# Buffers of a second matrix stage rotated in order of use, its memory laid out anew, weight preparation split in two

## The chip, the cores and the metric

The kernel runs on one core of one Trainium2 chip. The metric is the time of one execution in device microseconds, from the first to the last work of that core; a kernel's time is the median of its runs. Lower is better. Engines are named as in the profile: PE (matrix engine; PEld is its weight load), DVE (vector), ACT (scalar), POOL (GpSimd), SP (the engine that issues the transfers).

## The reference

An attention over pooled keys and values feeds two feed-forward layers. Both layers have 4608 tokens, a model width of 512 and a hidden width of 2048; they differ in the function between their two matrix products.

```python
def reference(q, k, v, ...):
    k_p, v_p = mean over groups of 8 rows of k, v          # (8, 8, 72, 64)
    attn = softmax(q @ k_p.T / sqrt(64)); x = attn @ v_p    # -> (4608, 512)
    h = x @ moe_w_in                                        # (4608, 2048)
    g = where(h >= 1, h, where(h <= -1, 0, (h + 1) ** 2 / 4))
    x = g @ moe_w_out                                       # (4608, 512)
    h = x @ moe2_w_in
    g = h - tanh(h)
    return g @ moe2_w_out                                   # (4608, 512)
```

## The kernel before

Every matrix operand is held as a pair, a rounded high part and the rest as a low part, and a product is three matmuls (high by high, high by low, low by high) added up in PSUM.

**First part.** The tokens go through in 12 blocks of 384. A block has 16 steps, one for each 128 hidden rows: `h_mm` makes the hidden values, DVE and ACT apply the function and split the result into `gh` and `gl`, and `out_mm` adds their product, two steps later, into four PSUM banks. Beside that run the attention of later blocks (names `pkt`, `psc`, `pam`, `ah`, `al`, `rr`; `al` is a DVE subtraction that frees the PSUM buffer that `pkt` and others use next) and, in steps of 8, `w2_prep`, which prepares the weights of the second layer. For an even unit, POOL forms four sums `c1` to `c4` of quarters of the first weight matrix, ACT and DVE split sums and quarters into high and low (L237, L238), and DMAs write them to memory as `w2c`; an odd unit gives `w2o`. The order of this part's engines is found by a scheduler that places the instructions by its own estimate of when they can run; POOL, ACT, DVE and SP each work off their queue strictly in that order.

**Second part.** 9 blocks J of 512 tokens by 8 pairs p of 256 hidden rows make 72 steps n = 8J + p. The first matrix product of a step is done in seven products of quarter size (`product(n, m)`, six matmuls of 256 columns each, in the order m = 1, 6, 7, 2, 5, 4, 3) into three PSUM banks `bkA`, `bkX`, `bkZ`. ACT and DVE combine them (`v_s`, `v_w`, `v_z`, `v_c11`, `v_t`, `v_c22`, `v_c21`, `v_c12`) into two halves: half 1 is complete after product 4, half 0 after product 3. On each half follow `v_th` (tanh, ACT), `v_sub` (DVE), `v_hi` (high part `gh`, ACT) and `v_lo` (low part `gl`, DVE), and `o_mm(n, half)`, 12 matmuls of 512 columns that add to the output banks `y0` to `y3`. `o_mm` of step n - 1 stands in PE's queue between the products of step n: half 1 before product 3, half 0 after it.

The order of the second part is a table of times (`at_time`) that is sorted; times are only the sorting key. `c`, `gh` and `gl` have three buffers each, and half h of step n takes buffer (2n + h) mod 3, while in every step half 1 is made and used first. So `v_hi(n, 1)` writes the buffer that half 0 of step n - 1 has, since (2n + 1) and 2(n - 1) differ by 3, and waits until `o_mm(n - 1, 0)`, the last matmuls of step n on PE, have read it.

Loads of the second part stand in SP's one queue: `xr` (the tokens of a block, converted by `xc_hi` on ACT and `xc_lo` on DVE into seven operands `xc`), `wc0` to `wc7` (1792 KB each, product weights of pair p, loaded once) and `wr` (512 KB each, weights of one `o_mm`, four buffers). Its memory is one pool per tag, laid out in the order of `LAYOUT` over the memory of the first part, and each tile waits only for those tiles of the first part that lie where it lies.

## Time and profile before

| what | us |
|---|---|
| median of 3 runs | 2015.25 (2009.29 to 2019.15) |
| the profiled execution | 2020.92 |
| its span, first to last instruction | 2018.8 |
| end of the first part on PE | about 992 |
| PE busy in the span | 1821.6 (90%) |

All rows below are from the one profiled execution, and their times count from its first instruction. The granted clock (PEclk) is 1.00 when TensorE had 2.4 GHz and 0.50 when it had 1.2 GHz for the whole stretch. A row of the timeline gives start, duration, engine, line, and in brackets the idle time ahead with what ended it. Durations of matmuls include the time in which their result drains, so that rows that follow each other overlap; the distance between starts is what PE spends.

### The profile page before, as it was taken

The numbers are of one execution on the slowest core, as the hardware profiler recorded it, in microseconds if no ns is written. First come the engines' busy times: TensorE is split into PE (matmuls) and PEld (weight loads), VectorE is DVE, ScalarE is ACT, GpSimd is POOL, SyncE is SP. The second block draws the span as 40 slices with busy tenths as digits, with TensorE's granted clock in tenths as the row PEclk, the third lists the DMA queues.
The fourth block names the chain that finished last, engine by engine and source line by source line (L and its number), as shares of the span: only waits on it lengthen the run. The fifth ranks groups of instructions, "written<-read, shape, count | busy, mean of one in ns | idle before, by whom it ended". The sixth has DMA issues, their size and how long they took to land.

```text
span 2018.8 us, 27653 instructions
## 1 busy us (share of the span) xinstructions
PE 1821.6 (90%) x10224; PEld 1657.9 (82%) x10224; DVE 1060.2 (53%) x1993; ACT 804.0 (40%) x2014; POOL 333.1 (17%) x433
## 2 busy tenths in 40 slices
PE   8999999999999999999858888888888888888888
PEld 6579999999999999999847777777777777777776
DVE  8878667666667665554413434343433334343433
ACT  6656555555555544443312323232322223232322
POOL 4442333223331242011010101001010101000000
PEclk8999999999999999999979999899989899999899
DMA  7623334233343231102362323123232323232222
GB/s 229 235 75 111 119 93 149 69 97 128 100 122 95 85 114 50 24 10 74 140 236 84 109 79 125 63 94 113 71 120 73 115 84 105 84 125 73 94 75 71
DMA packets 162423, 207.60 MB, mean 103 GB/s; under 512 B 77808, under 2 KB 115696, under 8 KB 161264
## 3 DMA queue, kind: packets, MB, share of 16 engines
q1 hardware_dynamic: 162288, 205.84, 31.4%
q8 instruction: 80, 1.31, 0.3%
q14 instruction: 55, 0.45, 0.1%
HBM read 163.32 MB, written 41.94 MB: 102 GB/s over the span
## 4 chain that ended last, share of the span: by engine, by line
PE 69%; DVE 12%; ACT 10%; DMA 3%; issue 3%; POOL 2%; SPq 0%; ACTq 0%; DVEq 0%; POOLq 0%
PE y L986 20%; PE po L617 15%; PE ph L572 14%; PE bkX L921 7%; ACT gh L970 4%; PE bkZ L921 3%; PE bkA L921 3%; DVE gl L974 3%; DVE c L964 2%; ACT th L961 2%; DMA wr<-w2o 2%; PE psc L431 2%; PE ph L565 1%; DVE c L957 1%; DVE gl L596 1%
## 5 line engine op out<-in xcount | busy, mean ns | idle before, releaser
L986 PE MATMUL y<-wr,gh 128*128 128x512 f32 x1152 | 370.1, 403 | 22.5 <-DMA wr<-w2o 22.0
L974 DVE TENSOR_TENSOR gl<-c,gh 128x512 fp32r<-128x512 f32 x144 | 104.2, 724 | 412.0 <-ACT gh L970 412.0
L921 PE MATMUL bkA<-xc,wc 128*128 128x256 f32 x864 | 144.3, 307 | 142.3 <-ACT s L933 140.7
L986 PEld LDWEIGHTS y<-wr,gh 128*128 128x128 f32 x1152 | 214.4, 196 | 63.2 <-DMA wr<-w2o 22.2
L921 PEld LDWEIGHTS bkA<-xc,wc 128*128 128x128 f32 x864 | 125.3, 202 | 163.3 <-ACT s L933 155.3
L970 ACT ACTIVATE gh<-c 128x512 fp32r<-128x512 f32 x144 | 90.8, 631 | 421.0 <-PE y L986 365.6
L986 PE MATMUL y<-wr,gl 128*128 128x512 f32 x576 | 229.2, 398 | 0.0
L921 PE MATMUL bkX<-xc,wc 128*128 128x256 f32 x1296 | 217.7, 309 | 3.0 <-DVE c L943 1.2
L921 PEld LDWEIGHTS bkX<-xc,wc 128*128 128x128 f32 x1296 | 194.4, 212 | 20.1 <-DVE c L943 12.8
L572 PE MATMUL ph<-xh,whl 128*128 128x384 f32 x704 | 200.3, 345 | 0.0
L583 ACT ACTIVATE g<-g,half 128x384 f32<-128x384 f32 x192 | 118.6, 618 | 199.6 <-DVE g L579 195.4
L617 PE MATMUL po<-gh,whl 128*128 128x384 f32 x704 | 196.7, 340 | 0.0
L961 ACT ACTIVATE th<-c 128x512 f32<-128x512 f32 x144 | 91.0, 632 | 245.1 <-DVE c L954 162.4
L596 DVE TENSOR_TENSOR gl<-g,gh 128x384 fp32r<-128x384 f32 x176 | 113.7, 646 | 81.7 <-ACT gh L595 79.4
L888 POOL TENSOR_TENSOR xr<-xr 128x512 f32<-128x512 f32 x9 | 11.6, 1290 | 863.7 <-DMA xr<-x2d 863.7
L964 DVE TENSOR_TENSOR c<-c,th 128x512 f32<-128x512 f32 x144 | 99.8, 693 | 99.8 <-ACT th L961 99.8
L579 DVE TENSOR_SCALAR g<-ph 128x384 f32<-128x384 f32 x192 | 106.2, 553 | 77.4 <-PE ph L572 70.7
L921 PE MATMUL bkZ<-xc,wc 128*128 128x256 f32 x864 | 146.2, 312 | 0.0
L587 DVE TENSOR_TENSOR g<-ph,g 128x384 f32<-128x384 f32 x192 | 106.4, 554 | 70.7 <-ACT g L583 68.7
L921 PEld LDWEIGHTS bkZ<-xc,wc 128*128 128x128 f32 x864 | 134.3, 224 | 0.0
L986 PEld LDWEIGHTS y<-wr,gl 128*128 128x128 f32 x576 | 110.2, 191 | 27.6 <-DVE gl L974 0.9
L572 PEld LDWEIGHTS ph<-xh,whl 128*128 128x128 f32 x704 | 130.9, 191 | 0.3
(156 smaller groups left out, 3642.2 us busy)
## 6 DMA issues: line engine op xcount, KB each, us to landing
wr<-w2o SPq DMA_DIRECT2D x144, 512.0 KB, 3.3
wraw<-in_moe_w_in_dram SPq DMA_DIRECT2D x32, 512.0 KB, 3.8
wraw<-in_moe_w_out_dram SPq DMA_DIRECT2D x32, 512.0 KB, 4.5
wc<-w2c SPq DMA_DIRECT2D x8, 1792.0 KB, 11.3
x2d<-ost SPq DMA_DIRECT2D x48, 192.0 KB, 1.9
out_dram<-yo SPq DMA_DIRECT2D x36, 256.0 KB, 2.2
w2c<-wraw SPq DMA_DIRECT2D x16, 512.0 KB, 2.6
kvraw<-in_k_dram SPq DMA_DIRECT2D x28, 256.0 KB, 2.8
```

The lines of the kernel that those rows point to most:

```text
L572: nc.tensor.matmul(ps, a[:, cs], x[:, c, :], start=(i == 0), stop=(i == 3 * KC - 1))
L579: nc.vector.tensor_scalar(a, hp[t], -1.0, 1.0, ALU.max, ALU.min)
L583: nc.scalar.activation(a, a, AF.Square, bias=half, scale=0.5)
L587: nc.vector.tensor_tensor(a, hp.pop(t), a, ALU.max)
L596: nc.vector.tensor_tensor(gl, a, gh.bitcast(F32), ALU.subtract)
L617: nc.tensor.matmul(o, a, m, start=(f == 0 and i == 0), stop=(f == FC - 1 and i == len(ops) - 1))
L921: nc.tensor.matmul(o, w[:, wi, c], x[:, xi, c], start=new and i == 0, stop=i == 5, skip_group_check=not new)
L961: nc.scalar.activation(th, H[(n, i)], AF.Tanh)
L964: nc.vector.tensor_tensor(H[(n, i)], H[(n, i)], GG.pop((n, i, "t")), ALU.subtract)
L970: nc.scalar.activation(gh, H[(n, i)], AF.Copy)
L974: nc.vector.tensor_tensor(gl, H.pop((n, i)), gh.bitcast(F32), ALU.subtract)
L986: nc.tensor.matmul(Y[c], a[:, cs], b, start=first and i == 0, stop=last and i == 2)
```

## The change

The rotation index of `c`, `gh` and `gl` becomes (2n + 1 - h) mod 3. `LAYOUT` puts the tags in another order, so that each lies over other tiles of the first part. The times at which `xr`, `wc`, `wr` and the first conversions are sorted in are new. `w2_prep` ends after POOL's sums, a new `w2_split` with the split and the DMAs follows two steps later, and the load of the next unit comes one step after that. As built, the seven `xc` now lie over first-part weights of hidden rows 8 to 11 (128 rows each), and their first conversions stand ahead of the last two steps' `gh` on ACT and `gl` on DVE; `wc0` lies over the constants, among them `half`, which every step's Square (L583) reads.

```diff
--- before.py
+++ after.py
@@ -231,6 +231,18 @@
             conv(r[:, i], a[:, i], r[:, i, :, 0])
         af = a.bitcast(F32)
         r0, r1 = (r[:, i].rearrange("p m t -> p (m t)") for i in (0, 1))
+        U[("w2", u)] = (r, af, r0, r1)
+        if u % 2:
+            return
+        a11, a12, a21, a22 = (af[:, i, 256 * c : 256 * c + 256] for i in (0, 1) for c in (0, 1))
+        c1, c2, c3, c4 = (r0[:, 256 * i : 256 * i + 256].bitcast(F32) for i in range(4))
+        nc.gpsimd.tensor_tensor(c1, a21, a22, ALU.add)
+        nc.gpsimd.tensor_tensor(c3, a11, a21, ALU.subtract)
+        nc.gpsimd.tensor_tensor(c2, c1, a11, ALU.subtract)
+        nc.gpsimd.tensor_tensor(c4, a12, c2, ALU.subtract)
+
+    def w2_split(u):
+        r, af, r0, r1 = U.pop(("w2", u))
         p = u // 2
 
         def split(x, hi):
@@ -244,12 +256,6 @@
                 nc.sync.dma_start(out=w2o[2 * p + i][:, 0], in_=hi)
                 nc.sync.dma_start(out=w2o[2 * p + i][:, 1], in_=lo)
             return
-        a11, a12, a21, a22 = (af[:, i, 256 * c : 256 * c + 256] for i in (0, 1) for c in (0, 1))
-        c1, c2, c3, c4 = (r0[:, 256 * i : 256 * i + 256].bitcast(F32) for i in range(4))
-        nc.gpsimd.tensor_tensor(c1, a21, a22, ALU.add)
-        nc.gpsimd.tensor_tensor(c3, a11, a21, ALU.subtract)
-        nc.gpsimd.tensor_tensor(c2, c1, a11, ALU.subtract)
-        nc.gpsimd.tensor_tensor(c4, a12, c2, ALU.subtract)
         split(af.rearrange("p i m -> p (i m)"), r1)
         for x, h in ((af.rearrange("p i m -> p (i m)"), 1), (r1.bitcast(F32), 0)):
             nc.sync.dma_start(out=w2c[p][:, h, 4:6], in_=x[:, 0:512].rearrange("p (m n) -> p m n", n=256))
@@ -805,7 +811,8 @@
             ahead("w", w_load, (1, f))
         t = FC + 8 * f + 5
         add(t, "w", w2_prep, f)
-        add(t + 1, "load2", used, "w")
+        add(t + 2, "w", w2_split, f)
+        add(t + 3, "load2", used, "w")
 
     def go(t, *slots):
         for s in slots:
@@ -847,8 +854,8 @@
     NPR = FC // 2
     TAGS = {}
     LAYOUT = (
-        "xc0 xc1 xc2 s0 s1 z0 w3 w4 r0 p640 w0 xc3 xc4 t0 w1 gh0 gh1 gh2 gl0 gl1 gl2 c0 c1 c2 xc5 t1"
-        " y0 y1 y2 y3 p1024 xr p1728 w6 w7 r1 w2 w5 r2 r3 xc6"
+        "w0 s0 p640 xc0 xc5 xc6 xc1 xc4 xc3 xc2 s1 z0 c0 w1 w2 r0 c1 c2 gh0 gh1 gh2 gl0 gl1 gl2 t0 t1 w5"
+        " y0 y1 p1024 xr p1728 w6 w7 y2 y3 w3 w4 r1 r2 r3"
     )
     for x in LAYOUT.split():
         TAGS[x] = one_pool(f"two_{x}", reuse_waits="tile")
@@ -925,7 +932,7 @@
 
     def tile_of(n, half):
         if (n, half) not in H:
-            H[(n, half)] = two(f"c{(2 * n + half) % 3}", [P, T2], F32, "c")
+            H[(n, half)] = two(f"c{(2 * n + 1 - half) % 3}", [P, T2], F32, "c")
         return H[(n, half)]
 
     def v_s(n):
@@ -964,7 +971,7 @@
         nc.vector.tensor_tensor(H[(n, i)], H[(n, i)], GG.pop((n, i, "t")), ALU.subtract)
 
     def v_hi(n, i):
-        k = (2 * n + i) % 3
+        k = (2 * n + 1 - i) % 3
         gh = two(f"gh{k}", [P, T2], F32R, "gh2")
         GG[(n, i)] = (gh, two(f"gl{k}", [P, T2], F32R, "gl2"))
         nc.scalar.activation(gh, H[(n, i)], AF.Copy)
@@ -1005,18 +1012,16 @@
     L = 10.4
     NS = NJ * NPR
     WHEN = {1: 0.0, 6: 0.7, 7: 1.4, 2: 2.1, 5: 2.8, 4: 3.5, 3: 6.95}
-    at_time(-60, xr_load, 0)
-    for i, p in enumerate((0, 1)):
-        at_time(-50 + i, wc_load, p)
-    at_time(-48, xr_sums, 0)
-    for i, m in enumerate(ORDER):
-        at_time(-47 + i, xc_hi, 0, m)
-        at_time(-46.5 + i, xc_lo, 0, m)
-    for i, p in enumerate(range(2, NPR)):
-        at_time(-30 + 4 * i, wc_load, p)
     fs = [2 * (n % NPR) + h for n in range(NS) for h in (1, 0)]
-    for i in range(4):
-        at_time(-5 + i, wr_load, fs[i])
+    at_time(-85, xr_load, 0)
+    at_time(-70, xr_sums, 0)
+    for p, t in enumerate((-80, -60, -55, -44, -34, 0, 8, 22)):
+        at_time(t, wc_load, p)
+    for i, t in enumerate((-54, -29, -28, -27)):
+        at_time(t, wr_load, fs[i])
+    for m, t in zip(ORDER, (-22, -21, -16, -15, -11, -10, -6)):
+        at_time(t, xc_hi, 0, m)
+        at_time(t + 0.6, xc_lo, 0, m)
     for n in range(NS + 1):
         J, p = divmod(n, NPR)
         b = n * L
```

ACT in a middle step of the second part, from `v_s` to the next step's `v_s`, with the engines that each row waits for. Before:

```order
L933 ACTIVATE s<-bkA 128x256 [waits PE_49]
L937 ACTIVATE z<-bkZ 128x256 [waits PE_49]
L940 ACTIVATE c<-bkA 128x256 [waits PE_49]
L961 ACTIVATE th<-c 128x512 [waits DVE_49,Activation_49]
L970 ACTIVATE gh_11746<-c 128x512 [waits DVE_49,PE_49]
L961 ACTIVATE th<-c 128x512 [waits DVE_49,Activation_49]
L970 ACTIVATE gh_11774<-c 128x512 [waits DVE_49]
L933 ACTIVATE s<-bkA 128x256 [waits PE_49]
```

After:

```order
L940 ACTIVATE s<-bkA 128x256 [waits PE_49]
L944 ACTIVATE z<-bkZ 128x256 [waits PE_49]
L947 ACTIVATE c<-bkA 128x256 [waits PE_49,Activation_49]
L968 ACTIVATE th<-c 128x512 [waits DVE_49]
L977 ACTIVATE gh_11746<-c 128x512 [waits DVE_49]
L968 ACTIVATE th<-c 128x512 [waits DVE_49,Activation_49]
L977 ACTIVATE gh_11774<-c 128x512 [waits DVE_49,PE_49]
L940 ACTIVATE s<-bkA 128x256 [waits PE_49]
```

The wait of the first `gh` (half 1) for PE has moved to the second `gh` (half 0).

SP from the load of `wc0` on, at the end of the first part (`x2d11` are the first part's last stores). Before, with the four first `wr` loads behind the last row shown:

```order
L868 DMA wc0_10510<-w2c0_84 128x3584 [waits DMAHW7_49,PE_49]
L627 DMA x2d11_119<-ost_10358 128x384 [waits DMAHW0_49,Activation_49]
L627 DMA x2d11_119<-ost_10358 128x384 [waits DMAHW1_49,DVE_49]
L627 DMA x2d11_119<-ost_10358 128x384 [waits DMAHW2_49,Activation_49]
L627 DMA x2d11_119<-ost_10358 128x384 [waits DMAHW3_49,DVE_49]
L868 DMA wc1_10512<-w2c1_85 128x3584 [waits DMAHW4_49]
L868 DMA wc2_10539<-w2c2_86 128x3584 [waits DMAHW5_49,PE_49]
L868 DMA wc3_10541<-w2c3_87 128x3584 [waits DMAHW6_49,PE_49]
L868 DMA wc4_10543<-w2c4_88 128x3584 [waits DMAHW7_49,PE_49]
L868 DMA wc5_10545<-w2c5_89 128x3584 [waits DMAHW0_49]
L868 DMA wc6_10547<-w2c6_90 128x3584 [waits DMAHW1_49,PE_49]
L868 DMA wc7_10549<-w2c7_91 128x3584 [waits DMAHW2_49,PE_49]
```

After:

```order
L875 DMA wc0_10510<-w2c0_84 128x3584 [waits DMAHW7_49,Activation_49]
L633 DMA x2d11_119<-ost_10358 128x384 [waits DMAHW0_49,Activation_49]
L633 DMA x2d11_119<-ost_10358 128x384 [waits DMAHW1_49,DVE_49]
L633 DMA x2d11_119<-ost_10358 128x384 [waits DMAHW2_49,Activation_49]
L633 DMA x2d11_119<-ost_10358 128x384 [waits DMAHW3_49,DVE_49]
L875 DMA wc1_10516<-w2c1_85 128x3584 [waits DMAHW4_49,PE_49]
L875 DMA wc2_10518<-w2c2_86 128x3584 [waits DMAHW5_49,PE_49]
L914 DMA wr_10520<-w2o1_93 128x1024 [waits DMAHW6_49]
L875 DMA wc3_10522<-w2c3_87 128x3584 [waits DMAHW7_49,PE_49]
L875 DMA wc4_10524<-w2c4_88 128x3584 [waits DMAHW0_49,PE_49]
L914 DMA wr_10526<-w2o0_92 128x1024 [waits DMAHW1_49]
L914 DMA wr_10528<-w2o3_95 128x1024 [waits DMAHW2_49,PE_49]
```

`wr` loads stand between the `wc` loads now, and `wc0` waits for ACT, the engine of the first part's last reader of its memory, instead of PE.

DVE in the first part around an even unit of `w2_prep` (L238 before, L250 after, is the split's subtraction; `g` and `gl` belong to the step's function). Before:

```order
L238 TENSOR_TENSOR wf<-wf,wraw 128x1024 [waits Activation_49,Pool_49]
L596 TENSOR_TENSOR gl<-g,gh 128x384 [waits Activation_49]
L579 TENSOR_SCALAR g<-ph 128x384 [waits PE_49]
L587 TENSOR_TENSOR g<-ph,g 128x384 [waits Activation_49]
L596 TENSOR_TENSOR gl<-g,gh 128x384 [waits Activation_49]
L579 TENSOR_SCALAR g<-ph 128x384 [waits PE_49]
L238 TENSOR_TENSOR wraw<-wraw 128x1024 [waits Activation_49]
L587 TENSOR_TENSOR g<-ph,g 128x384 [waits Activation_49]
L504 CAST ar_132<-par 16x128 [waits Activation_49]
L511 TENSOR_TENSOR al<-pam,ah 128x384
```

After:

```order
L250 TENSOR_TENSOR wf<-wf,wraw 128x1024 [waits Activation_49,Pool_49]
L602 TENSOR_TENSOR gl<-g,gh 128x384 [waits Activation_49]
L585 TENSOR_SCALAR g<-ph 128x384 [waits PE_49]
L593 TENSOR_TENSOR g<-ph,g 128x384 [waits Activation_49]
L602 TENSOR_TENSOR gl<-g,gh 128x384 [waits Activation_49]
L585 TENSOR_SCALAR g<-ph 128x384 [waits PE_49]
L517 TENSOR_TENSOR al<-pam,ah 128x384 [waits Activation_49]
L593 TENSOR_TENSOR g<-ph,g 128x384 [waits Activation_49]
L510 CAST ar_132<-par 16x128 [waits Activation_49]
L250 TENSOR_TENSOR wraw<-wraw 128x1024 [waits Activation_49]
```

The first subtraction, with its wait for POOL, stands where it stood; the second has moved behind `al`.

## Rows read from the trace of the kernel before

**Rows 1.** The page, busy time of PE: busy, share of the span, instructions.
```profile
PE 1821.6 (90%) x10224; PEld 1657.9 (82%) x10224; DVE 1060.2 (53%) x1993; ACT 804.0 (40%) x2014; POOL 333.1 (17%) x433
```

**Rows 2.** Stretches: length, then busy time (instructions) of PE, PEld, DVE, ACT, POOL; granted clock, DMA share, GB/s.
```profile
350.00:400.00 50.00, 50.00 (x300) 49.58 (x299) 32.20 (x66) 24.52 (x77) 13.56 (x20) 1.00 0.20 56
483.00:486.00 3.00, 3.00 (x11) 3.00 (x11) 1.39 (x5) 1.07 (x4) 1.22 (x4) 0.50 0.44 156
1010.00:1020.00 10.00, 0.00 (x0) 0.00 (x0) 0.00 (x0) 0.00 (x0) 0.00 (x0) 0.60 1.01 429
```

**Rows 3.** Waits of PE from 150 to 900: for whom, total us, times, longest.
```profile
PE pkt L350 <- DVE al L511: 12.2, 8, 2.8
PE psc L431 <- DVE al L511: 2.5, 2, 2.3
```

**Rows 4.** Timeline of DVE from 236 to 248, an even unit: start, us, what, [idle before].
```profile
237.32 1.23 DVE L238 TENSOR_TENSOR wf<-wf,wraw 128x1024 fp32r<-128x1024 f32 x1 [3.41 <-POOL wraw L252]
243.21 1.22 DVE L238 TENSOR_TENSOR wraw<-wraw 128x1024 fp32r<-128x1024 f32 x1
245.24 0.56 DVE L511 TENSOR_TENSOR al<-pam,ah 128x384 fp32r<-128x384 f32 x1
```

**Rows 5.** Timeline of SP's queue at the change of parts.
```profile
993.01 3.82 SPq L868 DMA_DIRECT2D wc<-w2c  x7
996.88 12.60 SPq L907 DMA_DIRECT2D wr<-w2o  x4
```

**Rows 6.** Timelines of ACT and PE at the change of parts.
```profile
986.74 0.62 ACT L583 ACTIVATE g<-g,half 128x384 f32<-128x384 f32 x1 [2.49 <-DVE g L579]
991.92 3.22 ACT L895 ACTIVATE xc<-xr 128x512 fp32r<-128x512 f32 x6
1000.68 0.95 PE L921 MATMUL bkA<-xc,wc 128*128 128x256 f32 x6 [1.55 <-DMA wc<-w2c]
1029.22 1.22 PE L986 MATMUL y<-wr,gh 128*128 128x512 f32 x2 [21.99 <-DMA wr<-w2o]
1033.55 0.88 PE L921 MATMUL bkX<-xc,wc 128*128 128x256 f32 x6
```

**Rows 7.** The line of the wc loads: time from issue to landing.
```profile
DMA to landing us min/median/max: 7.0/11.3/20.4
```

**Rows 8.** Timeline of PE in a middle step of the second part.
```profile
1505.45 0.86 PE L921 MATMUL bkX<-xc,wc 128*128 128x256 f32 x6
1506.15 0.63 PE L986 MATMUL y<-wr,gh 128*128 128x512 f32 x2
1508.95 0.86 PE L921 MATMUL bkA<-xc,wc 128*128 128x256 f32 x6
1513.05 1.16 PE L921 MATMUL bkA<-xc,wc 128*128 128x256 f32 x6 [1.82 <-ACT s L933]
1514.06 1.65 PE L921 MATMUL bkX<-xc,wc 128*128 128x256 f32 x6
1516.79 0.77 PE L986 MATMUL y<-wr,gh 128*128 128x512 f32 x2
1523.23 0.87 PE L921 MATMUL bkA<-xc,wc 128*128 128x256 f32 x6
```

**Rows 9.** Timeline of ACT in the same step.
```profile
1523.20 0.63 ACT L970 ACTIVATE gh<-c 128x512 fp32r<-128x512 f32 x1 [5.02 <-PE y L986]
1526.37 0.63 ACT L970 ACTIVATE gh<-c 128x512 fp32r<-128x512 f32 x1 [0.76 <-DVE c L964]
1526.91 0.37 ACT L933 ACTIVATE s<-bkA 128x256 f32<-128x256 f32 x1
```

**Rows 10.** Waits of PE from 1110 to the end: for whom, total us, times, longest.
```profile
PE bkA L921 <- ACT s L933: 129.6, 65, 2.8
```

**Rows 11.** Groups of DVE from 1100 to 1900: count, then busy us, mean ns of one, idle before.
```profile
L964 DVE TENSOR_TENSOR c<-c,th 128x512 f32<-128x512 f32 x116 | 80.4, 693 | 78.6 <-ACT th L961 78.6
L957 DVE TENSOR_TENSOR c<-bkX,s 128x256 f32<-128x256 f32 x58 | 24.2, 417 | 0.0
```

**Rows 12.** Timeline of PE: first product of steps 2 and 71, and the last matmul.
```profile
1037.06 0.86 PE L921 MATMUL bkA<-xc,wc 128*128 128x256 f32 x6
1993.67 0.87 PE L921 MATMUL bkA<-xc,wc 128*128 128x256 f32 x6
2014.69 0.39 PE L986 MATMUL y<-wr,gl 128*128 128x512 f32 x1
```

## Prediction

> **What bounds the kernel now.** I read the page first, then stretches of the span, then in each part what PE waits for. PE is busy 90% of the span [rows 1], so the question is where the other tenth lies and what PE spends at half clock. There are three places. In the first part PE is almost never idle and its clock stays at 1.00 (2.4 GHz) where it is not [rows 2]; its waits from 150 to 900 are nearly all for one subtraction, `al`, 12.2 + 2.5 us, the longest 2.8 [rows 3], and after such a wait the clock falls to 0.50 (1.2 GHz) [rows 2]. At the change of parts PE waits 21.99 us for the first `wr`, with no matmul at all from 1010 to 1020 while the transfers run at 429 GB/s [rows 2, 6]. In the second part, the largest place, PE waits 129.6 us in 65 of the steps for `s` on ACT [rows 10], and the clock falls again after these waits.
>
> **One step of the second part.** The period of the step shown is 1523.23 - 1508.95 = 14.28 us [rows 8]. From starts at full clock, a product costs 1506.15 - 1505.45 = 0.70 and an `o_mm` 1508.95 - 1506.15 = 2.80, so the matmuls of a step need 7 x 0.70 + 2 x 2.80 = 10.50. The rest is the wait of 1.82 before the second matmul group of `bkA`, and the half clock behind it: 1516.79 - 1514.06 = 2.73 for two products that need 1.40. Why is `s` late? ACT could make it 0.86 after the step's start, when the first product has drained, but in its queue stand `gh` of half 1, tanh and `gh` of half 0 of the step before. That first `gh` waited 5.02 us for PE, until 1523.20 [rows 9], which is the end of the last `o_mm` (1523.23 is the next start, [rows 8]): it wants the buffer that this `o_mm` reads. From there a chain of `gh`, `gl`, `c12`, tanh, `v_sub`, `gh` runs to 1526.91, when `s` starts, and PE stands. It closes every step: the period is the PE work up to the last `o_mm` plus this chain. From step 2 to step 71 the mean is (1993.67 - 1037.06) / 69 = 13.86 [rows 12].
>
> **The rotation, part by part.** With the index (2n + 1 - h) mod 3 the buffers follow each other in the order of use, and the writer of one meets the user three halves back. I walk one step from its start at 0, with 0.15 for the draining of a product (0.86 against 0.70, [rows 8]), 0.63 for tanh and `gh`, 0.37 for `s` [rows 9], 0.69 for a DVE subtraction of 512 columns and 0.42 for one of 256 [rows 11]. Six products start at 0, 0.70, 1.40, 2.10, 2.80, 3.50; `o_mm` of half 1 at 4.20, product 3 at 7.00, `o_mm` of half 0 at 7.70, next step at 10.50. `s` 0.86 to 1.23, wanted by the fourth product at 2.10. `w` 1.56 to 1.98, wanted at 2.80. `t` ends at 4.08, wanted at 7.00. `c22` ends at 4.50, `c21` at 4.92, tanh 5.55, subtraction 6.24, `gh` of half 1 at 6.87: its buffer was last read by an `o_mm` that ended at 0. `gl` 7.56. Product 3 drained at 7.85, `c12` 8.27, tanh 8.90, subtraction 9.59, `gh` of half 0 at 10.22: its wait for PE is new, but that `o_mm` ended at 7.00, so it costs nothing. Behind it in ACT's queue is the next `s`, wanted at 10.50 + 0.86 = 11.36: 1.1 us to spare. `gl` ends at 10.91 on DVE, where the next `w` is wanted at 12.06: 1.1 to spare. Nothing is late next; PE is the bound, and without its waits the clock should stay where it is from 350 to 400, at 1.00 with PE busy for all 50 us [rows 2]. So 10.50 a step. The slack is what hides two extra loads: in each block's last step seven conversions on ACT and seven on DVE (0.54 each on ACT, 3.22 for six, [rows 6]; on DVE at most 0.69), in its first step two copies on each. They bring the margins near zero, and POOL's sums slow DVE at times; I allow 6 us for the 8 changes of block. Gain: 69 x (13.86 - 10.50) = 232 less 6 = **226**. Bounds: 240 (nothing of the allowance and 0.1 less a step) and 200 (0.35 more a step, a third of the slack used up as waiting). Behind step 71 PE now needs 2014.69 + 0.39 - 1993.67 = 21.4 [rows 12]; it will need 10.50 + 2 x 2.80 = 16.1: **5.3** more.
>
> **The change of parts.** Seven `wc` are issued from 993.01 and the four `wr` behind them [rows 5]; `wc1` is there when PE goes on at 1000.68, the first `wr` at 1029.22 [rows 6]. Between lie 6 x 1792 + 512 = 11264 KB in 28.54 us, 395 KB a us, and they come in the order of their issue. After the change the first `wr` has one `wc` between it and `wc1`: 2304 KB, 5.8 us, at 1006.5. PE has the six products of step 1 until about 1007.5 (step 0 has no `o_mm` that would cover its chain, as before), so this wait is gone. The second `wr` has two more `wc` ahead: 4096 KB, 10.4 us, at 1016.9. That is the next late thing: the first `o_mm` and product 3 end near 1011, PE stands about 6 us, and at half clock the `o_mm` then takes the 1033.55 - 1029.22 = 4.3 that the first one took after its long wait [rows 6]; bounds 2.8 and 4.5. Step 2 starts at 1016.9 + 4.3 = 1021.2 instead of 1037.06 [rows 12]: **15.9**. Two edits cost here. `wc0`, loaded long before until now, waits for the last Square, which ends at 987.36 [rows 6] and will be up to 1.2 later for the conversions in front of it; 7.0 us to landing alone [rows 7] gives 994.4 to 995.6, against a start of step 0 near 992. What hides it: step 0 used to stand for its conversions (six on ACT from 991.92 to 995.14, [rows 6]), which are now done in the last steps of the first part beside matmuls, and step 1 waits for `wc1` anyway. Without that cover it would cost 3.6. The conversions themselves, seven on each of two engines that idle there, delay the last `gl` by a few tenths. The later `wc5` to `wc7` are wanted from step 5 on, 30 us after step 2, and cost nothing.
>
> **Weight preparation.** At the even unit shown DVE stands 3.41 us for POOL's sum, then subtracts until 238.55; later a second subtraction (243.21, 1.22 long) stands ahead of `al` at 245.24, for which PE waits 2.8 [rows 3, 4]. Four such waits, three of 2.8 and one of 2.3, make 10.7 of the 14.7 [rows 3]. The order of the changed kernel leaves the first subtraction and its wait for POOL where they were, although its call is two steps later; only the second goes behind `al`, with its ACT half. So `al` can have the second one's place at 243.21, 2.0 earlier; but `pkt` is moved ahead of four matmuls that PE used to do before it waited, so PE's wait also begins earlier, and about half of each remains. I take 5 for four waits and 3 for the half clock that follows them: **8**. Bounds 0 (POOL's moved rows make new waits; two places put its `kvraw` sums ahead of `rr`, at most 0.5 each) and 16 (all four waits and their clock).
>
> **The sum.** 226 + 5.3 + 15.9 + 8 = 255.2 from 2020.92 gives 1765.7 for an execution like the profiled one, which lies 0.28% above the median of the runs; the median then is 1765.7 x 2015.25 / 2020.92 = **1761**.
>
> **Rivals.** First, short waits that remain. If a conversion, a DVE-POOL conflict or an unforeseen order leaves a short wait in most steps, the clock swings. Rows: 1.33 us lost by two products at half clock after a wait of 1.82. With that alone in every step: 69 x 1.33 = 92 more, 1853. The Trainium skill ("TensorE: Matmul & The Clock Gate", section "A second HAM failure mode: psum-queue depth-cycling") says that short idles between groups of matmuls, while PSUM banks are cycled, can be enough to let the clock swing between its levels. By that rule the new loop, which cycles three banks, would be in this case; the trace shows the swing only behind waits. Against it stands the slack of 0.8 or more at each of the walk's joints. Chance 0.08.
>
> Second, transfers that share instead of queueing. If `wc5`, `wc6` and the next block's `xr` (2 x 1792 + 1024 = 4608 KB, 11.7 us), issued behind the second `wr`, took bandwidth from it, it would land that much later: 1773. The first `wr` now waits for all seven `wc` ahead of it and lands as the sum of their bytes says, which speaks against. The Trainium skill ("DMA: Bandwidth & Descriptors", section "Queues, rings and completion order") says that completion is not first in, first out per issuing engine, though each transfer engine consumes its ring in order; the trace agrees with the second half. Chance 0.05, inside the range.
>
> Third, the rotation does not do what it says: another wait of the same length ends last, and the period stays at 13.86. Then 1761 + 226 + 5 = 1992. For it: `gh` of half 0 has got a wait for PE. Against: 3.2 us between that `o_mm`'s end and the writer. Chance 0.03.
>
> Fourth, slower than before. Without waits PE is busy for 750 us on end; if the chip did not grant the full clock to that, a step of 10.50 at 1.00 would take 10.50 divided by the granted mean. It loses to the old kernel from a step of 13.86 + (5.3 + 15.9 + 8) / 69 = 14.28 on, a mean of 0.74; at 1.2 GHz throughout, 21.0, the kernel would take some 2490. For it: PE has never run this mix without pauses. Against: the first part is without pauses and at 1.00 [rows 2]. Chance 0.01.
>
> **How the numbers follow.** The forecast has 0.82, the rivals 0.08, 0.05, 0.03 and 0.01, and 0.01 is for a time within 0.5% of before, about what a measurement of this kernel can tell from no change. Faster 0.98, same 0.01, slower 0.01. Range: from 1761 the terms' ends are -14 and +26 (steps), -1.5 and +12 (change of parts, with the second rival), -8 and +8 (first part). They hardly come all together: **1743 to 1790**.
>
> **What would show it.** Right: PE's waits for `s` gone, steps 10.5 apart, granted clock 0.98 or more from 1050 on, the first `gh` waiting for DVE alone; one wait for `wr` of about 6 us near 1011 and none of 22; step 0 starting with a wait for `wc0`; waits for `al` about half as long. Wrong: a wait for ACT or DVE in most steps, steps at block changes over 12 us, a clock below 0.95 in the second part, or a wait for `wr` above 10 us.

## Result, and the profile after

The changed kernel takes 1777.41 us (median of 4 runs, 1774.08 to 1779.2) beside 2015.57 us for the kernel before (4 runs on the same chip, 2009.29 to 2019.15): a ratio of 0.8819, 95% interval 0.8793 to 0.8846. The profiled execution took 1774.08 us with a span of 1772.3; the one of before 2020.92 with 2018.8. So 246.5 us of span went, and the rows below say where from. The forecast was 1761, with a range of 1743 to 1790.

The page of after, to be held against [rows 1]: the busy line, and the 40 slices of PE and of the granted clock.

```profile
PE 1726.8 (97%) x10224; PEld 1591.2 (90%) x10224; DVE 1075.9 (61%) x1993; ACT 820.1 (46%) x2014; POOL 335.3 (19%) x433
...
PE   8999989999999999999999899999999999999999
...
PEclk8999999999999999999999899999999999999999
```

PE does the same 10224 matmuls in 95 us less busy time, since fewer of them run at half clock. The only two slices below 9 behind the start are one in the first part and the one of the change of parts. Stretches of after (length, then busy time and instructions of PE, PEld, DVE, ACT, POOL; granted clock, DMA share, GB/s):

```profile
995.00:1024.00 29.00, 21.50 (x111) 19.91 (x112) 9.32 (x19) 7.14 (x14) 0.00 (x0) 0.76 1.01 414
1024.00:1756.00 732.00, 732.00 (x4585) 657.49 (x4584) 381.96 (x696) 290.55 (x558) 45.18 (x32) 1.00 0.39 130
```

In the second part PE is busy for all of 732 us at a granted clock of 1.00 (2.4 GHz). The wait for `s` of [rows 10], 129.6 us in 65 steps, has no successor: from 1060 to the end the view of waits has no row for PE at all. The first product of step 2 and that of step 71, which answer to [rows 12]:

```profile
1023.65 0.88 PE L928 MATMUL bkA<-xc,wc 128*128 128x256 f32 x6
...
1752.26 0.87 PE L928 MATMUL bkA<-xc,wc 128*128 128x256 f32 x6
```

The mean step is (1752.26 - 1023.65) / 69 = 10.56 us where it was 13.86, and from step 71 to the end of the span are 20.0 us where there were 25.1. At the change of parts, where before showed a wait of 21.99 us for `wr` [rows 6], the timeline of PE now has these places (start, us, what, [idle before, and what ended it]), and that of SP's queue the issues below them, to be held against [rows 5]:

```profile
994.07 0.34 PE L623 MATMUL po<-gh,wl 128*128 128x384 f32 x1
...
999.26 1.01 PE L928 MATMUL bkA<-xc,wc 128*128 128x256 f32 x3 [4.85 <-DMA wc<-w2c]
...
1003.27 1.45 PE L928 MATMUL bkA<-xc,wc 128*128 128x256 f32 x6
1006.77 0.88 PE L928 MATMUL bkA<-xc,wc 128*128 128x256 f32 x6
1012.32 1.65 PE L928 MATMUL bkA<-xc,wc 128*128 128x256 f32 x6 [3.23 <-ACT s L940]
```

```profile
990.08 0.32 SPq L875 DMA_DIRECT2D wc<-w2c  x1
993.40 1.97 SPq L633 DMA_DIRECT2D x2d<-ost  x4
995.46 1.37 SPq L875 DMA_DIRECT2D wc<-w2c  x2
996.87 0.66 SPq L914 DMA_DIRECT2D wr<-w2o  x1
999.59 0.81 SPq L875 DMA_DIRECT2D wc<-w2c  x2
1000.46 1.81 SPq L914 DMA_DIRECT2D wr<-w2o  x3
```

The first row is the last matmul of the first part. `wc0` goes out only at 990.08, behind the last Square, and PE waits 4.85 us for it, then runs the first four products at half clock (1.45 for the fourth instead of 0.88). Step 1 waits 3.23 us for ACT's chain of step 0 and goes on at half clock too (1.65). No `wr` is waited for in this execution; in several of the runs below there is such a wait. From the last matmul of the first part to step 2 it is 1023.65 - 994.07 = 29.6 us; before it was 1037.06 - 991.68 = 45.4.

And the first part did not become shorter: its last matmul starts at 994.07, where that of before started at 991.68. PE's waits from 150 to 900, against [rows 3] (for whom, total, times, longest):

```profile
PE pkt L356 <- DVE al L517: 16.1, 10, 3.1
PE ppv L537 <- DVE ar L510: 4.1, 7, 0.9
```

The waits for `al` grew from 12.2 us in 8 to 16.1 in 10, and there is a new one, for `ar`. So the 246.5 us are 228.0 in the steps (69 x 3.304), 5.1 behind step 71, 15.8 at the change of parts, and -2.4 in the first part.

### The profile page after: what moved, and what is told of

Read it like the earlier page. It is cut to its first block, busy times and chain, and to the rows that moved or that the text cites. A ratio compares the mean times of both kernels' runs of the same rounds, so it can differ in the third digit from the quotient of the medians.

```text
span 1772.3 us, 27599 instructions
## 1 busy us (share of the span) xinstructions
PE 1726.8 (97%) x10224; PEld 1591.2 (90%) x10224; DVE 1075.9 (61%) x1993; ACT 820.1 (46%) x2014; POOL 335.3 (19%) x433
## 4 chain that ended last, share of the span: by engine, by line
PE 76%; DVE 10%; DMA 5%; ACT 4%; POOL 3%; issue 2%; SPq 1%; ACTq 0%; DVEq 0%; POOLq 0%
PE y L993 23%; PE po L623 14%; PE ph L578 14%; PE bkX L928 9%; PE bkA L928 6%; PE bkZ L928 6%; DMA wraw<-in_moe_w_out_dram 2%; DVE gl L602 1%; PE psc L437 1%; DVE wf L166 1%; DVE g L585 1%; DVE wf L250 1%; DVE wraw L164 1%; POOL kvraw L315 1%; PE ph L571 1%
## 5 line engine op out<-in xcount | busy, mean ns | idle before, releaser
L993 PE MATMUL y<-wr,gh 128*128 128x512 f32 x1152 | 362.1, 395 | 0.0
L993 PEld LDWEIGHTS y<-wr,gh 128*128 128x128 f32 x1152 | 206.9, 188 | 39.6
L928 PE MATMUL bkX<-xc,wc 128*128 128x256 f32 x1296 | 189.8, 282 | 0.0
L928 PEld LDWEIGHTS bkX<-xc,wc 128*128 128x128 f32 x1296 | 175.0, 190 | 6.0
L928 PE MATMUL bkA<-xc,wc 128*128 128x256 f32 x864 | 127.7, 284 | 8.1 <-DMA wc<-w2c 4.8
L928 PEld LDWEIGHTS bkA<-xc,wc 128*128 128x128 f32 x864 | 119.0, 192 | 15.0 <-DMA wc<-w2c 5.2
L623 PEld LDWEIGHTS po<-gh,whl 128*128 128x128 f32 x704 | 128.8, 188 | 0.0
L601 ACT ACTIVATE gh<-g 128x384 fp32r<-128x384 f32 x176 | 91.9, 522 | 78.0 <-PE po L623 55.3
```

Of the source, the lines that this page charges most:

```text
L601: nc.scalar.activation(gh, a, AF.Copy)
L623: nc.tensor.matmul(o, a, m, start=(f == 0 and i == 0), stop=(f == FC - 1 and i == len(ops) - 1))
L928: nc.tensor.matmul(o, w[:, wi, c], x[:, xi, c], start=new and i == 0, stop=i == 5, skip_group_check=not new)
L993: nc.tensor.matmul(Y[c], a[:, cs], b, start=first and i == 0, stop=last and i == 2)
```

## Experiments

### The buffer index alone, and all but the index

The kernel before with the new index alone:

```
-            H[(n, half)] = two(f"c{(2 * n + half) % 3}", [P, T2], F32, "c")
+            H[(n, half)] = two(f"c{(2 * n + 1 - half) % 3}", [P, T2], F32, "c")
...
-        k = (2 * n + i) % 3
+        k = (2 * n + 1 - i) % 3
```

> The kernel before with the new buffer index (2n+1-h in tile_of and v_hi) and nothing else: old memory layout, old load times, weight preparation in one stage. Theory: the index alone takes the bkA-on-s wait away, so the step of the second part falls from 13.86 to about 10.56 us and the tail from 25.1 to about 20.0 us, while step 2 still begins near 1037; that is 228 + 5 = 233 us less, about 1783 us (1775 to 1792), ratio to before 0.885. Rival: the rotation needs the new layout to work (a buffer or a weight load that the old layout frees late takes the place of the wait); then the step stays above 11 us and the time above 1810.

Measured: 1784.8 us, ratio 0.8852 (0.8821 to 0.8884). The step is (1765.16 - 1037.53) / 69 = 10.55 us. Of PE's waits at the change of parts the large one stands as before:

```profile
PE y L986 <- DMA wr<-w2o: 21.2, 1, 21.2
```

The changed kernel with these two lines put back:

> The changed kernel with the old buffer index and everything else kept (new layout, new load times, two-stage preparation). Theory: the step goes back to 13.86 us and the tail to 25.1, so 1777.4 + 233 = about 2010 us, ratio to before 0.997 (0.993 to 1.000): what is left is 13.4 us at the step-2 row, of which the first wr wait alone is the greater part. Rival: the load order or the layout is what shortened the step; then the time stays under 1900.

Measured: 2007.84 us, ratio 0.9962 (0.9937 to 0.9986). The step is 13.78 us again. The two runs lie within 3 us of their expectations, and their gains, 229.6 and 6.5 us against 2014.35 for before in the same series, add up to 236 of the 238 of the whole change. Old layout, old loads and old preparation do not hinder the rotation: its rival falls.

### Which of the two indices

The changed kernel with the old index for the `c` buffers only, then with the old index for `gh` and `gl` only:

```
-            H[(n, half)] = two(f"c{(2 * n + 1 - half) % 3}", [P, T2], F32, "c")
+            H[(n, half)] = two(f"c{(2 * n + half) % 3}", [P, T2], F32, "c")
```

> The changed kernel with the old index for the c buffers (tile_of) and the new one for gh and gl (v_hi). Theory: the wait came from gh, which v_hi(n,1) on ACT writes and the last o_mm of the step before still reads; the c buffer has long been read by then. So this index alone gives the whole step gain: 1777 us (1772 to 1783). Rival: the c index is needed as well (the subtraction of the step before still reads c(n-1,0) when the sum of step n wants to write c(n,1)); then the step stays above 11 us, over 1805 us.

```
-        k = (2 * n + 1 - i) % 3
+        k = (2 * n + i) % 3
```

> The changed kernel with the new index for the c buffers and the old one for gh and gl. Theory: nothing of the step gain is left, the step is 13.86 us again and the time that of the run without rotation, 2008 us (2000 to 2015). Rival: part of the wait came through c; then 1800 to 1980 us.

Measured: 1778.29 us with the `gh` index alone (step 10.56), and 2015.68 with the `c` index alone (step 13.90; ratio to before 1.000, 0.9968 to 1.0032). With the latter the wait of before is back in PE's timeline, here in step 71:

```profile
1990.38 0.87 PE L928 MATMUL bkA<-xc,wc 128*128 128x256 f32 x6
1994.47 0.95 PE L928 MATMUL bkA<-xc,wc 128*128 128x256 f32 x6 [1.81 <-ACT s L940]
```

So the whole step gain hangs on one line, which sets the buffers that `gh` and `gl` write. The two were not tried one by one; the row that waited 5.02 us for the last `o_mm` in [rows 9] is `gh` of half 1, and `gl` is made from it. The index of `c` is worth nothing that can be measured.

### Weight preparation in one stage again

```
-        add(t + 2, "w", w2_split, f)
-        add(t + 3, "load2", used, "w")
+        add(t, "w", w2_split, f)
+        add(t + 1, "load2", used, "w")
```

> The changed kernel with the weight preparation in one stage again (second stage in the same step as the first, the next load one step later, as before); rotation, layout and load times kept. Theory from the trace of after: the two stages cost the first part about 2.4 us (its last matmul came at 994.4 instead of 992.0), so 1775 us, 1 to 4 us under the changed kernel. The prediction on record says the opposite: two stages gain 8 us, so this would be 1785. Third: no difference beyond 1 us, the 2.4 us being what two executions differ by.

Measured: 1771.93 us, ratio 0.8791 (0.8763 to 0.8819), 5.5 us under the changed kernel; the last matmul of the first part starts at 991.16. The intervals of the two ratios overlap, so I also hold the profiles side by side. With one stage this row lies at 991.68, 991.16, 992.70, 991.40 and 989.83 in five profiles (before, this run, the index alone, and the two combined kernels below that have one stage and the tree on POOL); with two stages at 994.07, 1000.03, 1001.29, 996.36 and 999.58 (after, and four runs with after's first part). No value of the one group reaches the other; the means are 991.4 and 998.3. By these profiles two stages cost the first part some 7 us, by the medians 5.5, where the prediction counted 8 of gain.

Why? At the even unit the change did what was predicted: in after, `al` comes ahead of the second subtraction (rows of DVE and PE, against [rows 4]).

```profile
241.21 0.55 DVE L517 TENSOR_TENSOR al<-pam,ah 128x384 fp32r<-128x384 f32 x1
241.81 0.33 PE L356 MATMUL pkt<-ident,bd 128*128 128x128 f32 x1 [1.38 <-DVE al L517]
243.15 1.23 DVE L250 TENSOR_TENSOR wraw<-wraw 128x1024 fp32r<-128x1024 f32 x1 [0.24 <-ACT wraw L249]
245.71 0.44 PE L537 MATMUL ppv<-ar,vlr 128*128 128x384 f32 x1 [0.89 <-DVE ar L510]
```

PE's wait is 1.38 instead of 2.81, and the same at the two later units of this kind (1.38 and 1.37 instead of 2.81 and 2.82). But 0.89 comes back at once, because the subtraction now stands between two casts of `ar`, and the rest is given back 22 us later, where before had no wait:

```profile
252.28 0.19 DVE L461 RECIPROCAL rc<-sm 128x6 f32<-128x6 f32 x1
254.86 1.86 POOL L315 TENSOR_TENSOR kvraw<-kvraw 128x768 f32<-128x768 f32 x1 [0.25 <-DMA qr<-in_q_dram]
254.94 2.33 DVE L166 CUSTOM_DVE_ANT_0 wf<-wraw,wf 128x1024 uint16<-128x1024 uint16 x1
256.80 1.34 POOL L315 TENSOR_TENSOR kvraw<-kvraw 128x384 f32<-128x384 f32 x1
257.20 1.50 DVE L164 SCALAR_TENSOR_TENSOR wraw<-wraw 128x512 int32<-128x512 int32 x1
...
263.49 0.55 DVE L517 TENSOR_TENSOR al<-pam,ah 128x384 fp32r<-128x384 f32 x1
264.09 0.33 PE L356 MATMUL pkt<-ident,bd 128*128 128x128 f32 x1 [1.98 <-DVE al L517]
```

In the kernel before, at the same unit, the reciprocal of the softmax stood amid the conversion and POOL's adding tree over `kvraw` began when most of the conversion was done:

```profile
257.15 0.19 DVE L455 RECIPROCAL rc<-sm 128x6 f32<-128x6 f32 x1
257.34 0.69 DVE L164 SCALAR_TENSOR_TENSOR wraw<-wraw 128x512 int32<-128x512 int32 x1
259.62 0.69 DVE L166 CUSTOM_DVE_ANT_0 wf<-wraw,wf 128x1024 uint16<-128x1024 uint16 x1
259.92 4.73 POOL L309 TENSOR_TENSOR kvraw<-kvraw 128x768 f32<-128x768 f32 x3 [0.19 <-issue]
```

In after the reciprocal is ahead of the conversion, the tree starts 5 us earlier and lies upon it. The rows of the two engines interlock: DVE's L166, begun 0.08 behind POOL's first add, takes 2.33 instead of 0.69 and ends 0.55 behind the add's end at 256.72. The wait of 1.98 comes again as 1.97 at 504 and 1.78 at 743, and two waits that before had as well grew from 1.25 to 2.74 (at 346) and from 1.26 to 3.14 (at 586). Whether the tree is the cause needed runs of its own.

### Without POOL's tree

```
-        tree(eng, kvraw)
```

> The changed kernel with the adding tree over kvraw on POOL (three adds for each head pair of keys and values from the second token block on) left out, so that keys and values are not averaged over their 8 rows there. Theory for the loss in the first part: in two stages the softmax sums on DVE come ahead of the next unit's conversion, POOL's tree starts some 5 us earlier and now runs beside the conversion, whose rows grow (wraw shift-and-or 912 ns on average instead of 704, the custom row 825 instead of 682), and `al` is late behind them. Without the tree these rows fall back to about 690 ns, the waits near 264, 504 and 743 (1.97 us each) go, and the first part ends 6 us or more earlier than in the changed kernel: about 1769 us (1764 to 1773). Rival: the rows grow for another reason (DMA writes, ACT), or `al` is late only by its place in DVE's order; then they stay and the time is 1776 to 1778.

Measured: 1751.0 us, ratio 0.8697 (0.8668 to 0.8725): 26 us under the changed kernel, not 8. The last matmul of the first part starts at 969.23. PE's waits of `pkt` for `al` fall from 16.1 us to 2.5, the longest 1.4: those at 264, 504 and 743 are gone. The wait of some 0.85 for `ar` behind each even unit stays. So the direction was right and the size far off: in two stages the tree costs 26 us altogether, far more than the 5.5 by which two stages are slower than one.

At the unit of the wait of 1.98 the trace shows the price row by row. DVE has the same rows in the same order, from a reciprocal at 245.34 on (252.28 in after):

```profile
248.02 0.68 DVE L166 CUSTOM_DVE_ANT_0 wf<-wraw,wf 128x1024 uint16<-128x1024 uint16 x1
248.63 0.68 DVE L164 SCALAR_TENSOR_TENSOR wraw<-wraw 128x512 int32<-128x512 int32 x1
254.10 0.54 DVE L516 TENSOR_TENSOR al<-pam,ah 128x384 fp32r<-128x384 f32 x1
```

L166 and L164 are 1.65 and 0.82 us shorter than in after, 2.47 together, and `al` begins 8.76 us behind the reciprocal instead of 11.21, 2.45 earlier. So at this unit the two stretched rows are the whole delay, more than PE's wait of 1.98.

To separate the tree from the two stages, one stage without the tree:

> One-stage weight preparation with rotation and new layout, and with POOL's adding tree over kvraw left out in the same way as in the run before it (two stages without the tree: 1751.0 us, last matmul of the first part at 969.2). With the tree, two stages cost 5.5 us (1777.4 against 1771.9). Theory: they cost it because they bring the tree beside the conversion on DVE; without the tree the loss is gone or turns into the gain that the prediction counted, so one stage without the tree takes 1751 to 1758 us. Rival: the loss lies in DVE's own order (the second half sits between the casts of `ar`); then one stage is again about 5.5 us faster, 1745 to 1746.

Measured: 1759.09 us, ratio 0.8718 (0.8703 to 0.8734). Without the tree two stages are 8.1 us faster than one by the medians; with it, 5.5 us slower. The sign turns, as the theory said, and the rival (a loss in DVE's own order) would have given 1745 to 1746. The sizes are less sure than the sign. The intervals of the two ratios overlap, and the ratios, 0.8718 and 0.8697, give 4 us rather than 8. But the four times of two stages (1749.35 to 1757.05) all lie below the four of one (1758.82 to 1759.93), and the last matmul of the first part starts at 969.23 against 976.10. The groups of DVE from 150 to 900 (busy us, mean ns of one, idle before), for after, then one stage, then without the tree in two stages and in one:

```profile
L164 DVE SCALAR_TENSOR_TENSOR wraw<-wraw 128x512 int32<-128x512 int32 x30 | 27.3, 912 | 2.9 <-ACT wraw L159 2.6
L166 DVE CUSTOM_DVE_ANT_0 wf<-wraw,wf 128x1024 uint16<-128x1024 uint16 x32 | 26.4, 825 | 0.4
```

```profile
L164 DVE SCALAR_TENSOR_TENSOR wraw<-wraw 128x512 int32<-128x512 int32 x30 | 21.0, 703 | 6.0 <-DMA kvraw<-in_v_dram 3.1 <-ACT wraw L159 2.9
L166 DVE CUSTOM_DVE_ANT_0 wf<-wraw,wf 128x1024 uint16<-128x1024 uint16 x32 | 21.8, 682 | 0.2
```

```profile
L164 DVE SCALAR_TENSOR_TENSOR wraw<-wraw 128x512 int32<-128x512 int32 x30 | 22.2, 742 | 3.5 <-ACT wraw L159 3.1
```

```profile
L164 DVE SCALAR_TENSOR_TENSOR wraw<-wraw 128x512 int32<-128x512 int32 x30 | 21.0, 704 | 9.3 <-ACT wraw L159 9.3
```

The conversion's rows grow by 20% and more only where two stages and the tree meet (742 instead of 704 ns without the tree). The tree's loss takes other things with it: `pkt` can be ready earlier, and POOL has more time for its sums `c1` to `c4`. So the runs show that the tree is behind the turn of the sign, and at the unit above that stretched rows are the delay, not that every microsecond of the 26 is one. That the tree only holds up those sums doesn't give the sign: from 150 to 900 DVE's subtraction waits 14.1 us for them in one stage and 11.8 in two with the tree, 5.9 and 4.2 without it, less in two stages either way.

### `wc0` loaded early

`half`, a constant of four bytes that the last Square reads, lies in the memory that `wc0` takes. Here it is declared last in its pool, outside of it:

```
-    half = const.tile([P, 1], F32, tag="half", name="half")
...
     ars = [const.tile([P, TB], F32R, tag=f"ar{i}", name=f"ar{i}") for i in range(2)]
+    half = const.tile([P, 1], F32, tag="half", name="half")
```

> The changed kernel with the small constant `half` placed last in its pool instead of third, out of the memory that wc0 takes. The load of wc0 then no longer waits for the last Square and goes out near 933 instead of 990.1. Theory: the 4.85 us wait of the first product and most of the half clock behind it go, but wc1 is still queued behind the last x2d writes (issued 995.5), so step 1 begins when wc1 lands, near 1003 to 1004 instead of 1006.8: 2 to 4 us less, about 1774. Rival: step 1 is held by wc1 to the same point and the standing TensorE falls to half clock there instead, so nothing is gained (1777). Rival: wc1 lands much earlier as the only transfer in flight, and 6 us or more are gained (1771).

Measured: 1780.17 us, ratio 0.8831 (0.8805 to 0.8857): no difference from the changed kernel. `wc0` goes out at 940.01, and the 4.85 us are gone, but PE's timeline shows what takes their place:

```profile
1001.29 0.34 PE L623 MATMUL po<-gh,wl 128*128 128x384 f32 x1
1001.47 0.87 PE L928 MATMUL bkA<-xc,wc 128*128 128x256 f32 x6
...
1010.38 1.62 PE L928 MATMUL bkA<-xc,wc 128*128 128x256 f32 x6 [3.71 <-ACT th L968]
...
1026.14 1.22 PE L993 MATMUL y<-wr,gh 128*128 128x512 f32 x2 [5.22 <-DMA wr<-w2o]
1030.69 0.88 PE L928 MATMUL bkA<-xc,wc 128*128 128x256 f32 x6
```

From the first row to step 2 it is 29.4 us, where after has 29.6, and the medians show no gain: the rival that foresaw none is right. (Three other runs with the loads and first part of after have 31.6 to 32.2 there; a gain of some 2 us against those would lie within what the medians differ by.) Step 1 stands 3.71 us. The row names a tanh of ACT, on which that product doesn't depend; its `wc1` was issued at 1002.66 behind the last `x2d` writes, and 7.7 us to landing is what the row [rows 7] allows, so I read it as `wc1`. Then PE stands 5.22 for the second `wr`, which has `wc1` to `wc4` ahead of it in the queue.

### The queue put in the order of need

One stage, `half` moved, and the first two `wr` directly behind `wc1`:

```
-    for i, t in enumerate((-54, -29, -28, -27)):
+    for i, t in enumerate((-59, -58, -28, -27)):
```

> The rotation and the new layout with one-stage weight preparation, `half` out of wc0's memory, and the first two wr loads placed right behind wc1, ahead of wc2, wc3 and wc4. Theory: at the change of parts each removed wait was covered by the next transfer in SP's queue (in the run with `half` moved alone the 4.85 us wait for wc0 became 3.7 us in step 1 and 5.2 us for wr). With wc0 early and wr third in the queue both go: step 1 begins about 9 us after the last matmul of the first part (wc1), step 2 some 14 to 15 us after that, near 1015 instead of 1022.0 in the one-stage run: 6 to 7 us less than its 1771.9, about 1765 us. Rival: what is taken from the wr wait comes back as a wait for wc2 or for the ACT chain of steps 0 and 1, at half clock; then the time stays at 1771 to 1772.

Measured: 1767.94 us, ratio 0.8771 (0.8751 to 0.879): 4 us under the run with one stage, not 6 to 7, and the intervals overlap. Step 2 begins at 1012.33 instead of 1022.02, but in step 3 PE waits for a later `wr`, which stood behind the next block's `xr` on SP:

```profile
1002.66 14.71 SPq L887 DMA_DIRECT2D xr<-x2d  x4
1017.75 7.12 SPq L914 DMA_DIRECT2D wr<-w2o  x2
```

```profile
1031.35 1.22 PE L993 MATMUL y<-wr,gh 128*128 128x512 f32 x2 [2.80 <-DMA wr<-w2o]
```

So both theory and rival had a part: part of the wait moved one load further. The same kernel with the load of `xr` later:

```
-            at_time(b + 1.1 * L, xr_load, J + 1)
+            at_time(b + 2.2 * L, xr_load, J + 1)
```

> The run with early wc0 and early wr (1767.9 us) with one thing more: the load of the next block's xr is issued 1.1 steps later (2.2 instead of 1.1 steps into each block), behind the wr loads of steps 1 and 2 in SP's queue and not ahead of them. Theory: xr waits on SP for its buffer (14.7 us in that run), the wr loads behind it were issued at 1017.75 and TensorE waited 2.80 us for one near 1031 and then ran at half clock; with the order turned round that goes: 3 to 4 us less, 1764 us. Rival: the xr load then comes with its sums too late for another stage, or the wr buffers are not free earlier anyway: 1768 or more.

Measured: 1763.62 us, ratio 0.8743 (0.8726 to 0.876), as the theory said; of PE's waits from 960 on one is left, 3.3 us for `wc1`. The interval overlaps that of the run before it, so neither of the two steps is clear of noise by itself; both together, 1771.93 to 1763.62, are.

### The tree on DVE, in one stage and in two

```
-        tree(eng, kvraw)
+        tree(nc.vector, kvraw)
```

> As the run with xr later, and the adding tree over kvraw on DVE instead of POOL. Without any tree the first part ended 25 to 32 us earlier in two stages. On DVE the three adds cost by their sizes (768, 384, 192 elements; 1024 elements took 1.22 us there) about 1.7 us a tree where POOL took 4.3 to 4.7 us, and no DVE row grows beside them any more. Theory: most of what the tree costs is POOL's hold on DVE's rows; 10 us or more are gained, 1754 us or less. Rival: DVE's queue is what `al` waits behind, and 1.7 us more in it for each head pair lengthen the waits: no gain or a loss, 1764 to 1775.

Measured: 1757.04 us, ratio 0.8714 (0.8696 to 0.8731): 6.6 us less than with the tree on POOL (the two intervals overlap by 0.0005), against 10 or more expected; what held the rest back was not looked into. On top of it two stages:

> The run with the adding tree on DVE (1757.0 us, one stage) with the weight preparation in two stages again. Without the tree two stages took 8.1 us less than one (1751.0 against 1759.1), with the tree on POOL 5.5 us more. Theory: what turns the sign is POOL's tree beside DVE's conversion rows; with the tree on DVE that is gone as well, so two stages gain up to 8 us, 1749 to 1755 us, and the conversion rows (wraw shift-and-or, 704 ns in one stage) stay under 760 ns. Rival: three more adds in DVE's own queue stand where the second stage now stands, and `al` is late behind them: 1757 to 1763.

Measured: 1753.99 us, ratio 0.8706 (0.869 to 0.8723), 23 us under the changed kernel and the fastest complete kernel here. Two stages now gain 3.0 us by the medians and 1.6 by the ratios, whose intervals overlap, so this pair alone does not settle the sign. It points the same way as the pair without the tree. In the profile the last matmul of the first part starts at 980.42 (one stage: 989.47, in an execution that lay 5 us above its median), and the waits from 150 to 900 answer to [rows 3]:

```profile
PE pkt L356 <- DVE al L517: 5.4, 10, 1.6
PE ppv L537 <- DVE ar L510: 4.9, 9, 0.9
```

DVE's L164 stays at 718 ns there. The first add of a tree takes 1074 ns on DVE on the mean, where it takes 1895 on POOL in after.

## Why the prediction was right, and where it was not

Point by point, in the order of its sum.

**The step.** Predicted 10.50 plus 6 us for block changes, that is 226; measured 10.56 on average, 228.0. The reading of the chain was right to the buffer: the run with the index of `gh` alone has the whole gain. No wait is left in any step, and the slack of about 1 us that the walk found is there: in this plain step, which starts at 1467.17, `gh` of half 0 of the step before has just ended, and ACT stands 0.91 us until the first product has drained.

```profile
1468.07 0.38 ACT L940 ACTIVATE s<-bkA 128x256 f32<-128x256 f32 x1 [0.91 <-PE bkA L928]
```

The 6 us for block changes were hardly needed: no stall shows at them, the longest steps are 10.64, and the 0.06 us above 10.50 are spread over all steps as matmul time, 4 us in 69. Behind step 71: 5.3 predicted, 5.1 measured.

**The change of parts.** 15.9 predicted, 15.8 measured (45.4 to 29.6), but in the profile of after not by the rows that it named. It put the whole rest into a 6 us wait for the second `wr`; in after there is none, and PE stands for `wc0` and `s` instead. `wc0`'s landing was mis-sized: it was issued at 990.08 in place of about 988, for the greater part because the first part ended 2.4 later, and took 9.1 us instead of 7.0. The other profiles with this order of loads do have the predicted wait, beside shorter ones for `wc0` and `s`. With the index of `gh` alone:

```profile
1022.99 1.22 PE L993 MATMUL y<-wr,gh 128*128 128x512 f32 x2 [4.84 <-DMA wr<-w2o]
```

It is 5.0 us without the rotation, 3.5 with the index of `c` alone, 3.4 in one stage and 5.2 with `half` moved. The forecast had the second `wr` at 1016.9, 25.2 us behind the start of the first part's last matmul at 991.68. PE starts on its matmuls 24.9 to 27.1 us behind that row in all six profiles (1020.75 - 994.07 = 26.7 in after, 1022.99 - 996.36 = 26.6 in the run above, 1026.14 - 1001.29 = 24.9 with `half` moved). So the reading that this load sets the length of the change of parts was right, and so was the statement that the wait for `wc0` is covered: what PE stands earlier it doesn't stand at the `wr`. The close match of 15.8 is luck of one execution. From the last matmul to step 2 it is 30.9 to 32.2 us in the four profiles that keep `wc0` late and have the wait, which makes the gain 13 to 14.5.

**Weight preparation.** This is the step that failed: 8 predicted with a lower bound of 0, about -6 measured (-2.4 between the two profiles, -5.5 between the medians). Half of each of the three long waits at even units did go (2.81 to 1.38). But the prediction followed only the rows that the change moves, and put a bound of "0.5 each" on POOL's sums that get ahead; it did not ask which DVE rows those sums would lie beside. They lay on the next unit's conversion, and PE paid 1.98 us for it at 264. With the tree away two stages do gain, 8.1 us by the medians, 4 by the ratios. That 8.1 is so near the predicted 8 is in part luck: without the tree the waits at even units are not three of 2.8 in one stage but 0.76, 2.93 and 1.05, so the term is not made up as the prediction had it.

**The sum.** By profiles, 246.5 of 255.2: 8.7 too much, of which 10.4 is the weight preparation and -1.7 the rest. The forecast of 1761 is 16 below the median of 1777.41; the other half of that is that the two profiled executions lay on different sides of their medians, that of before 5.4 us above, that of after 3.3 below. The profile of after showed the first part at the short end of its range (994 of 994 to 1001), and the change of parts shorter than in the four profiles named above (29.6 against 30.9 to 32.2). One profile told less of either than the prediction took from it.

**The rivals.** Short waits and a swinging clock did not come: the granted clock is 1.00 over 732 us. The Trainium skill ("TensorE: Matmul & The Clock Gate", section "A second HAM failure mode: psum-queue depth-cycling") names short idles of PE between groups of matmuls, in a loop that cycles PSUM banks, as what let the clock swing; this loop cycles three banks without idling, and the trace shows no swing, so the condition of idles is not met here. Half clock under a sustained load fell with the same row. Transfers that share, which were to bring the second `wr` 11.7 us later, did not come either: PE has it 24.9 to 27.1 us behind the last matmul, where the queue alone was forecast to take 25.2. That the rotation doesn't do what it says fell with the run of the index alone.

What is not settled: why the first part in two stages ends anywhere from 994 to 1001 in five profiles, when in one stage the range is 989.8 to 992.7. Rows of DVE and POOL that block each other could turn small shifts into large ones, but no run here tests that.

## What to carry to other kernels

Follow a wait back to the buffer that the waiting writer wants, and count how many uses lie between: with three buffers an index in the order of use, and not in the order of naming, was worth 230 of 238 us. When a transfer's wait is removed, look at what stands behind it in the same queue; a wait taken from the head of the queue came back further down until the order of issue was that of need. When work on DVE is moved, list what POOL does at the new place and where POOL's work itself goes, since a two-input row of DVE that met a POOL add here waited for its end.

## What the runs showed of the hardware

DVE and POOL took turns in the rows with two inputs that met. In after, POOL's add ran from 254.86 to 256.72, and DVE's L166, with two inputs, begun at 254.94, took 2.33 us where the same row takes 0.68 on the mean without the tree. POOL's next add, of 384 elements, ran from 256.80 to 258.14, and DVE's L164, begun at 257.20, took 1.50 us instead of 0.70 and ended 0.56 behind it. L165, with one input, met it too: one begun at 338.66, beside a POOL add begun at 338.08, took 1.60 us, and its mean from 150 to 900 is 529 ns in after against 438 in one stage. The Trainium skill ("SBUF — State Buffer", section "Who interferes with whom") says that a DVE instruction with two inputs in SBUF contends with a GpSimd instruction that reads SBUF, and calls the port pair that they share an exclusive lock; the trace agrees, 0.55 us from the add's end to the end of L166. What I had not expected is the sum: the three adds of a tree take 1.90, 1.20 and 0.73 us on the mean in after, 3.8 us of POOL's time for a head pair, POOL was busy for 19% of the span, and leaving the tree out took 26 us from the kernel in two stages and 13 in one (1771.93 to 1759.09).

PE ran 4585 matmuls in 732 us without a wait, at 1.00 throughout, on transfers of 130 GB/s. At the change of parts the transfer engines are at a share of 1.01 and 414 GB/s from 995 to 1024; issuing one of eight loads 50 us earlier (940.01 instead of 990.08) gained nothing there, and the same early load together with two changes of the order in the queue took 8 us off (1771.93 to 1763.62).
